# Experts' first layer from seven products for each pair of tiles and pair of blocks, in three passes over the weights

## The chip, the core and the metric

One core of a Trainium2 chip runs the whole program as one launch. The metric is the device time of an execution in microseconds (us). The engines are PE (TensorE: matmuls, with their weight loads shown apart as PEld), DVE (VectorE), ACT (ScalarE), POOL (GpSimd) and SP, which issues the DMAs. Each engine works through its own instructions in a fixed order, and semaphores tell it when an operand is there. PE writes into banks of PSUM, which DVE and ACT read. SBUF holds everything else.

## What is computed

An attention with a threshold, then a gated layer (three weight matrices), then eight dense experts under gates that are normalised over rows and columns in turn. The change is in the experts:

```python
def _moe2_ref(x, w_gate, w1, w2):            # x: 2304 x 512
    logits = x @ w_gate                      # 512 x 8
    P = np.exp(logits - logits.max())
    for _ in range(8):
        P /= P.sum(1, keepdims=True) + 1e-09
        P /= P.sum(0, keepdims=True) + 1e-09
        P *= N / E
    for e in range(E):                       # 8 experts
        h = np.maximum(x @ w1[e], 0.0)       # 512 x 1024
        ye = h @ w2[e]                       # 1024 x 512
        out += P[:, e:e + 1] * ye
```

## The kernel before

Tokens lie in 6 blocks of 384 columns (NBLK, BLK), and a block is 3 tiles of 128 tokens (NTB). A product in full precision is made of three matmuls in fp32r: each operand is split into a high part, which ACT copies (`copy_act`, line 194), and a low part, which DVE or POOL subtracts; `mm3` (lines 853 to 855) then adds high x high, high x low and low x high.

After attention comes the gated layer in `steps` (c, i): four chunks c of the hidden width by six blocks i, with `gate_val` and `down`. The output of block i of the last chunk is `x2[i]`, [128, 4, 384], and `down` splits it for the experts into `x2s[i]` (line 1019). `logits` and `logits_t` make the gates' logits from it.

The experts follow in `steps2`: the 8 x 8 hidden tiles of 128 features go in 24 groups g of three, three and two for each expert, and each group runs over all six blocks. Step (g, i) is `up` (for every hidden tile 12 matmuls of 384 columns into one bank of `ps_a`, a relu on ACT, line 1116, and the low part on DVE, line 1117) and then `mix` of the step before, so that PE does not wait for the relu. `mix` makes, for each of the 3 token tiles, 3 matmuls of 512 columns for every hidden tile of the group into one of the four banks of `ps_o`, and DVE adds the bank to `acc[i]` with the gate (line 1151; without a gate for expert 0, line 1147; where expert 0 is finished, line 1150 multiplies its sum by the gate once). All six `acc` stay in SBUF, and the weights of a group (`a{g}` of w1, `b{g}` of w2) are loaded once, two loads ahead, and split once by `w_step`, which is called between the steps: ACT copies the high part, POOL subtracts the low part (line 799).

`gate_steps` (lines 1071 to 1099) is a generator: it turns the logits into gates in short pieces of DVE work with one small PE matmul between two pieces (`mxT`, `mxB`, eight times `cs`). Two pieces go behind each step from the third step on.

Scratch in SBUF comes from slots of one size (`new`, `drop`, first free first taken).

## Time and profile before

| | |
|---|---|
| median of 3 runs | 2411.72 us (2410.64 to 2414.01) |
| the profiled execution, whole | 2410.57 us |
| its span, from the first to the last instruction | 2408.5 us |
| mean granted TensorE clock | 0.995 |
| PE busy / PEld | 2365.5 us (98%) / 2141.9 us (89%) |
| DVE / ACT / POOL busy | 1097.1 / 652.8 / 628.9 us (46 / 27 / 26%) |
| read from / written to HBM | 68.96 / 7.08 MB |

A page of the profile shows one execution. Matmuls are pipelined: the duration of one is longer than the distance from its start to the start of the next, and it is the distance that counts where they run without a gap. "Idle before" an instruction is time in which its engine had nothing to do. In the span, attention ends at about 350 us, the gated layer runs to about 800 us, and the experts take the rest.

### The profile page before, as it was taken

The numbers are of one execution on the slowest core, as the hardware profiler recorded it, in microseconds if no ns is written. First come the engines' busy times: TensorE is split into PE (matmuls) and PEld (weight loads), VectorE is DVE, ScalarE is ACT, GpSimd is POOL, SyncE is SP. The second block draws the span as 40 slices with busy tenths as digits, with TensorE's granted clock in tenths as the row PEclk, the third lists the DMA queues.
The fourth block names the chain that finished last, engine by engine and source line by source line (L and its number), as shares of the span: only waits on it lengthen the run. The fifth ranks groups of instructions, "written<-read, shape, count | busy, mean of one in ns | idle before, by whom it ended". The sixth has DMA issues, their size and how long they took to land.

```text
span 2408.5 us, 31221 instructions
## 1 busy us (share of the span) xinstructions
PE 2365.5 (98%) x12925; PEld 2141.9 (89%) x12925; DVE 1097.1 (46%) x1873; ACT 652.8 (27%) x1154; POOL 628.9 (26%) x601
## 2 busy tenths in 40 slices
...
DMA packets 94365, 107.40 MB, mean 45 GB/s; under 512 B 45200, under 2 KB 70800, under 8 KB 94224
## 3 DMA queue, kind: packets, MB, share of 16 engines
...
q14 instruction: 40, 0.33, 0.0%
HBM read 68.96 MB, written 7.08 MB: 32 GB/s over the span
## 4 chain that ended last, share of the span: by engine, by line
PE 90%; POOL 5%; issue 1%; DMA 1%; ACT 1%; DVE 1%; SPq 1%; POOLq 0%; DVEq 0%; ACTq 0%
PE h L853 11%; PE h L855 11%; PE h L854 11%; PE y L854 11%; PE y L855 11%; PE y L853 11%; PE d L854 2%; PE d L855 2%; PE d L853 2%; PE v L853 2%; PE v L854 2%; PE v L855 2%; PE g L853 2%; PE g L854 2%; PE g L855 2%; PE s L454 1%
## 5 line engine op out<-in xcount | busy, mean ns | idle before, releaser
L1116 ACT ACTIVATE hh<-h 128x384 fp32r<-128x384 f32 x384 | 188.8, 492 | 1194.8 <-PE h L855 1194.8
L1117 DVE SCALAR_TENSOR_TENSOR hl<-h,hh 128x384 fp32r<-128x384 f32 x384 | 213.9, 557 | 629.4 <-ACT hh L1116 629.3
L1151 DVE SCALAR_TENSOR_TENSOR acc<-y,gate_p,acc 128x512 f32<-128x512 f32 x378 | 283.9, 751 | 357.7 <-PE y L855 357.6
L478 DVE SCALAR_TENSOR_TENSOR em<-ns,st,ee 128x576 f32<-128x576 f32 x144 | 138.3, 960 | 12.6 <-POOL st L465 8.2
L990 POOL TENSOR_TENSOR al<-av,ah 128x384 fp32r<-128x384 f32 x72 | 88.2, 1226 | 179.2 <-ACT ah L194 179.2
L469 ACT ACTIVATE ee<-ns,st 128x576 f32<-128x576 f32 x144 | 111.6, 775 | 32.1 <-DVE ns L461 31.2
L454 PE MATMUL s<-kk,qs 128*128 128x288 f32 x512 | 99.8, 325 | 18.1 <-DMA kk<-khl 9.5
L461 DVE TENSOR_SCALAR_CACHE_REDUCE ns<-s 128x576 f32<-128x576 f32 x144 | 108.3, 752 | 17.2 <-PE s L454 11.2
L988 DVE TENSOR_TENSOR av<-v,s 128x384 f32<-128x384 f32 x72 | 40.0, 556 | 158.9 <-PE v L855 143.3
L454 PEld LDWEIGHTS s<-kk,qs 128*128 128x128 f32 x512 | 75.1, 197 | 38.6 <-DVE ns L461 13.8
L544 PE MATMUL t<-ident,em 128*128 128x128 f32 x576 | 85.6, 280 | 3.1 <-ACT et L194 2.2
L194 ACT ACTIVATE et<-t 128x512 f32<-128x512 f32 x144 | 83.3, 591 | 9.6 <-PE t L544 9.2
L465 POOL TENSOR_TENSOR st<-st,ntau 128x1 f32<-128x1 f32 x144 | 67.9, 471 | 53.4 <-DVE ns L461 52.0
L194 ACT ACTIVATE ah<-av 128x384 fp32r<-128x384 f32 x72 | 37.9, 526 | 158.8 <-DVE av L988 158.8
L544 PEld LDWEIGHTS t<-ident,em 128*128 128x128 f32 x576 | 67.9, 143 | 11.6 <-ACT et L194 5.3
L626 PE MATMUL pv<-et,rv 128*64 128x320 f32 (+1 forms) x512 | 73.7, 421 | 0.7 <-ACT raw_k L383 0.7
L1013 DVE TENSOR_TENSOR x<-d,x 128x384 f32<-128x384 f32 x72 | 39.4, 554 | 35.6 <-PE d L855 35.6
L986 ACT ACTIVATE s<-g 128x384 f32<-128x384 f32 x72 | 34.7, 482 | 75.3 <-PE g L855 75.3
L626 PEld LDWEIGHTS pv<-et,rv 128*64 128x64 f32 x512 | 33.2, 139 | 24.0 <-issue 6.5
L640 POOL TENSOR_TENSOR xT<-u,rb 64x64 f32<-64x64 f32 (+2 forms) x71 | 46.0, 661 | 4.4 <-ACT u L194 3.2
L1147 DVE TENSOR_TENSOR acc<-y,acc 128x512 f32<-128x512 f32 x36 | 24.9, 692 | 32.2 <-PE y L855 32.2
L1019 POOL TENSOR_TENSOR x2l<-x,x2h 128x1536 fp32r<-128x1536 f32 x6 | 21.0, 3503 | 24.6 <-ACT x2h L194 24.6
...
## 6 DMA issues: line engine op xcount, KB each, us to landing
...
raw_a<-in_moe_w_dram SPq DMA_DIRECT2D x16, 768.0 KB, 4.5
raw_b<-in_moe_w_dram SPq DMA_DIRECT2D x16, 768.0 KB, 4.6
...
raw_g<-in_moe_w_gate_dram SPq DMA_DIRECT2D x6, 768.0 KB, 4.7
raw_v<-in_moe_w_val_dram SPq DMA_DIRECT2D x6, 768.0 KB, 4.6
raw_o<-in_moe_w_out_dram SPq DMA_DIRECT2D x6, 768.0 KB, 4.4
...
```

The costliest lines, as they stand in the source:

```text
L194: nc.scalar.activation(out=o, in_=i, func=AF.Copy)
L454: nc.tensor.matmul(ps[:, n, 0:HS], lhs, rhs[:, ko + n * HS:ko + (n + 1) * HS], start=(x == 0), stop=(x == len(ops) - 1))
L461: nc.vector.tensor_scalar(x, sc[t], -1.0, None, op0=ALU.mult, op1=ALU.min, accum_out=stat[t][:, 0:1])
L469: nc.scalar.activation(out=ee[t], in_=sc[t], func=AF.Exp, bias=stat[t][:, 0:1], scale=-1.0)
L478: nc.vector.scalar_tensor_tensor(m, sc.pop(t), stat.pop(t)[:, 1:2], ee.pop(t), op0=ALU.is_le, op1=ALU.mult, accum_out=sums[p][:, s:s + 1],)
L544: nc.tensor.transpose(ps[:, kb * P:(kb + 1) * P], em[p, s // 2][:, o:o + P], ident)
L853: nc.tensor.matmul(ps, a[0], b[0], start=start, stop=False)
L854: nc.tensor.matmul(ps, a[0], b[1], start=False, stop=False)
L855: nc.tensor.matmul(ps, a[1], b[0], start=False, stop=stop)
L1116: nc.scalar.activation(out=hh[:, f], in_=t[:, 0:BLK], func=AF.Relu)
L1117: nc.vector.scalar_tensor_tensor(hl[:, f], t[:, 0:BLK], 0.0, hh[:, f].bitcast(F32), op0=ALU.max, op1=ALU.subtract)
L1151: nc.vector.scalar_tensor_tensor(a, t, gate_p[:, i * NTB + n, e:e + 1], a, op0=ALU.mult, op1=ALU.add)
```

## The change

The experts' first layer now takes two hidden tiles (256 features), two halves of d (2 x 256) and two blocks of tokens together as a product of 2 x 2 matrices, and makes it from seven products in the place of eight (`PARTS`). Each product is 6 matmuls of 384 columns (2 parts of d by the 3 of the split). Its operands are sums: of the weights s1 to s4 (`a_steps`, made anew in every pass on DVE and then split) and of the blocks t1 to t4 (`x_sums`). Some sums of products are made in PSUM, by letting a later product add to a bank whose contents ACT has copied out (`kept`); others on DVE (`hidden`, which adds a bank to a kept copy, so that relu and low part now read SBUF for three of the four tiles).

The loops turn inside out: a step k is one of 32 pairs of hidden tiles (NG) for one pair of blocks u, and there are three passes u = 0, 1, 2 over all weights, so 96 steps. Weights are loaded and split in each pass: `a_load(k + 2)` and `b_load(k)` issue five DMAs at the start of step k; `a_steps(k + 1)` and then `b_steps(k)` are handed out by `w_some` in pieces, two in each `between`. A `between` also issues one token tile of the `mix` of the step before (6 matmuls of 512 columns) and one piece of `gate_steps`. In a step PE thus runs products 1, 2, a token tile, 6, a tile, 5, a tile, 7, a tile, 4, 3 and two tiles. At the turn of a pass three tiles come right behind product 2 (`first`). The operands of the next pass are split in steps 29 and 61 (`x_first`, `x_second`) and summed and split in steps 31 and 63 (`x_sums`); those of the first pass inside the last chunk of the gated layer. Blocks 2 to 5 give their logits by plain fp32 matmuls; block 1 by 12 in the place of 8. Output is stored at the end of each pass.

```diff
-    groups = []
-    for e in range(E):
...
+    PAIRS = FE // P // 2
+    NG = E * PAIRS
...
-    for g, (e, f, n) in enumerate(groups):
...
-            for x in range(2):
-                nc.tensor.matmul(
-                    ps[0:2 * E, 0:BLK], gws[:, c].rearrange("p a e -> p (a e)"), x2s[i][x][:, c, :],
...
+        u, second = divmod(i, 2)
+        n = E if u else 2 * E
+        if u:
+            mms = [(gw[:, c], x2[i][:, c, :]) for c in range(CC)]
...
+    def x_op(u, nm, x, eng):
+        t = new([P, 2, 2, BLK], F32R, f"X{u}_{nm}")
+        xo[u, nm] = hi, lo = t[:, 0], t[:, 1]
+        copy_act(hi, x)
+        eng.tensor_tensor(lo, x, hi.bitcast(F32), op=ALU.subtract)
+    def x_first(u):
+        for nm, c in (("11", 0), ("21", 2)):
+            x_op(u, nm, x2[2 * u][:, c:c + 2, :], nc.gpsimd)
+    def x_second(u):
+        x_op(u, "22", x2[2 * u + 1][:, 2:4, :], nc.gpsimd)
+    def x_sums(u):
+        (b11, b21), (b12, b22) = ((x[:, 0:2, :], x[:, 2:4, :]) for x in x2[2 * u:2 * u + 2])
+        for nm, out, a, b in (("t1", b11, b12, b11), ("t3", b12, b22, b12), ("t2", b22, b22, b11), ("t4", b21, b21, b22)):
+            nc.vector.tensor_tensor(out, a, b, op=ALU.subtract)
+        for nm, x, eng in (("t2", b22, nc.vector), ("t1", b11, nc.gpsimd), ("t3", b12, nc.vector), ("t4", b21, nc.gpsimd)):
+            x_op(u, nm, x, eng)
+        drop(f"x2_{2 * u}")
+        drop(f"x2_{2 * u + 1}")
+    wa, wb, raws = {}, {}, {}
...
+    def a_load(k):
+        e, j = divmod(k % NG, PAIRS)
+        f = 2 * j * P
+        src = w1[e].rearrange("(c p) f -> p c f", p=P)
+        t = raws["a", k] = rw.tile([P, 6, 2, P], F32, tag="raw", name=f"a{k}")
+        nc.sync.dma_start(t[:, 0:2].rearrange("p a c f -> p (a c) f"), src[:, :, f:f + P])
+        nc.sync.dma_start(t[:, 2], src[:, 2:4, f + P:f + 2 * P])
+        nc.sync.dma_start(t[:, 3], src[:, 0:2, f + P:f + 2 * P])
...
+    def a_steps(k):
+        t = raws.pop(("a", k))
+        a11, a12, a22, a21 = (t[:, n] for n in range(4))
+        s1, s2, s3, s4 = t[:, 4], t[:, 5], a21, a12
+        one = new([P, 2, 3, 2, P], F32R, f"wa{k}")
+        two = new([P, 2, 3, 2, P], F32R, f"wb{k}")
+        three = new([P, 2, 2, P], F32R, f"wc{k}")
+        wa[k] = {"s4": (three[:, 0], three[:, 1])}
+        for n, (x, y) in enumerate((("11", "s3"), ("12", "s1"), ("22", "s2"))):
+            wa[k][x] = one[:, 0, n], one[:, 1, n]
+            wa[k][y] = two[:, 0, n], two[:, 1, n]
+        def split(hi, lo, x):
+            yield lambda: copy_act(hi, x)
+            yield lambda: nc.gpsimd.tensor_tensor(lo, x, hi.bitcast(F32), op=ALU.subtract)
+        def sums():
+            nc.vector.tensor_tensor(s1, a21, a22, op=ALU.add)
+            nc.vector.tensor_tensor(s2, s1, a11, op=ALU.subtract)
+            nc.vector.tensor_tensor(s3, a11, a21, op=ALU.subtract)
+        yield sums
+        yield from split(one[:, 0], one[:, 1], t[:, 0:3])
+        yield from split(two[:, 0], two[:, 1], t[:, 3:6])
+        yield lambda: nc.vector.tensor_tensor(s4, a12, s2, op=ALU.subtract)
+        yield from split(three[:, 0], three[:, 1], s4)
...
+    def b_load(k):
+        e, j = divmod(k % NG, PAIRS)
...
+        for n, t in enumerate(raws["b", k]):
+            nc.sync.dma_start(t, w2[e][f + n * P:f + (n + 1) * P, :])
...
+    def b_steps(k):
+        hi, lo = wb[k] = new([P, 2, DM], F32R, f"b{k}h"), new([P, 2, DM], F32R, f"b{k}l")
+        for n, t in enumerate(raws.pop(("b", k))):
+            yield lambda n=n, t=t: copy_act(hi[:, n], t)
+            yield lambda n=n, t=t: nc.gpsimd.tensor_tensor(lo[:, n], t, hi[:, n].bitcast(F32), op=ALU.subtract)
...
             if ip == NBLK - 1:
                 w_drop(f"o{cp}")
-        if c == NCH - 1 and i >= 2:
-            logits(i - 2)
+        if c == NCH - 1:
+            if i == 1:
+                x_first(0)
+            if i == 2:
+                x_second(0)
+                x_sums(0)
+            if i == 4:
+                a_load(0)
+                a_load(1)
+            if i == 5:
+                for fn in a_steps(0):
...
-    def up(g, i):
...
-            sl = slice(f * P, (f + 1) * P)
-            for d in range(CC):
-                mm3(t[:, 0:BLK], (wh[:, d, sl], wl[:, d, sl]), (xh[:, d, :], xl[:, d, :]), d == 0, d == CC - 1)
-            nc.scalar.activation(out=hh[:, f], in_=t[:, 0:BLK], func=AF.Relu)
-            nc.vector.scalar_tensor_tensor(hl[:, f], t[:, 0:BLK], 0.0, hh[:, f].bitcast(F32), op0=ALU.max, op1=ALU.subtract)
...
+    def up(k, u):
...
+        def mm(ps, n, start):
+            a, b = wa[k][PARTS[n][0]], xo[u, PARTS[n][1]]
+            for d in range(2):
+                (ah, al), (bh, bl) = ((x[:, d] for x in y) for y in (a, b))
+                nc.tensor.matmul(ps, ah, bh, start=start and d == 0, stop=False, skip_group_check=True)
+                nc.tensor.matmul(ps, ah, bl, start=False, stop=False, skip_group_check=True)
+                nc.tensor.matmul(ps, al, bh, start=False, stop=d == 1, skip_group_check=True)
...
+        def kept(ps, tag):
+            t = tmp.tile([P, BLK], F32, tag=tag, name=tag)
+            copy_act(t, ps)
+            return t
+        def hidden(nm, x, ps=None):
+            if ps is not None:
+                nc.vector.tensor_tensor(x, ps, x, op=ALU.add)
+            if nm in ("11", "22"):
+                for m in (nm, "21" if nm == "11" else "12"):
+                    hid[k, u, m] = hp_.tile([P, 2, BLK], F32R, tag="h", name=f"h{k}_{u}_{m}")
+            h = hid[k, u, nm]
+            nc.scalar.activation(out=h[:, 0], in_=x, func=AF.Relu)
+            nc.vector.scalar_tensor_tensor(h[:, 1], x, 0.0, h[:, 0].bitcast(F32), op0=ALU.max, op1=ALU.subtract)
+        a = bank()
+        mm(a, 1, True)
+        p1 = kept(a, "s")
+        yield
+        b = bank()
+        mm(b, 2, True)
+        hidden("11", p1, b)
+        yield
+        mm(a, 6, False)
+        u2 = kept(a, "av")
+        yield
+        c = bank()
+        mm(c, 5, True)
+        yield
+        mm(a, 7, False)
+        u3 = kept(a, "u3")
+        hidden("22", u3, c)
+        yield
+        mm(a, 4, False)
+        hidden("21", a)
+        yield
+        mm(c, 3, False)
+        hidden("12", u2, c)
+        yield
...
-    def mix(g, i):
...
+    def mix(k, u):
...
+            if g == 0 and n == 0:
...
-            for f in range(nf):
-                mm3(t, (hh[:, f, sl], hl[:, f, sl]), (wh[:, f], wl[:, f]), f == 0, f == nf - 1)
+            for f, h in enumerate(hs):
+                mm3(t, (h[:, 0, sl], h[:, 1, sl]), (wh[:, f], wl[:, f]), f == 0, f == 1)
...
-    steps2 = [(g, i) for g in range(NG) for i in range(NBLK)]
+                if n == NTB - 1:
+                    drop(f"acc{i}")
+            yield
+    steps2 = [(k, k // NG) for k in range(3 * NG)]
     sink = None
-    for n, (g, i) in enumerate(steps2):
-        for _ in range(2):
...
-        up(g, i)
...
-            logits_t(NBLK - 2)
...
+    def between(n):
+        nonlocal sink
+        x = next(fill, None)
+        if callable(x):
+            x()
+        w_some(n)
+        if sink is not None and next(sink, 0) == 0:
+            sink = None
+    for k, u in steps2:
+        if k + 2 < len(steps2):
+            a_load(k + 2)
+        b_load(k)
+        products = up(k, u)
+        fill = iter([down_last, lambda: logits(4)]) if k == 0 else mix(*steps2[k - 1])
+        if k + 1 < len(steps2):
+            w_parts.extend(a_steps(k + 1))
+        if k == 5:
+            while sink is not None:
+                between(0)
+        first = k and u > steps2[k - 1][1]
+        next(products)
+        next(products)
+        between(2)
+        if first:
+            between(1)
+            between(1)
+        next(products)
+        if not first:
+            between(2)
+        next(products)
+        between(2)
+        next(products)
+        between(2)
+        next(products)
+        next(products)
+        w_parts.extend(b_steps(k))
+        a_drop(k)
+        if k % NG == NG - 3 and u < 2:
+            x_first(u + 1)
+            x_second(u + 1)
+        if k % NG == NG - 1 and u < 2:
+            for nm in ("11", "21", "22", "t1", "t2", "t3", "t4"):
+                drop(f"X{u}_{nm}")
+            x_sums(u + 1)
+        between(2)
+        between(2)
+        w_some(99)
...
+            logits_t(4)
+        if k == 1:
+            logits_t(5)
             sink = gate_steps()
-        if sink is not None:
-            for _ in range(2):
-                if next(sink, 0) == 0:
-                    sink = None
-                    break
-    mix(*steps2[-1])
+    for _ in mix(*steps2[-1]):
+        pass
```

What is left out are the same edits elsewhere: hidden tiles of the gated layer are single tiles [128, 2, 384] of a pool of six, in the place of two tiles of three, and the weights of the experts are no longer in the list of `pieces`.

What stands in a row on DVE in the middle of the experts, ahead (`hl`: low part of a hidden tile; `acc`: a token tile is added):

```order
L1117 SCALAR_TENSOR_TENSOR hl12_1_14302<-h12_1_0_14303,hh12_1_14301 128x384
L1117 SCALAR_TENSOR_TENSOR hl12_1_14302<-h12_1_1_14318,hh12_1_14301 128x384
L1117 SCALAR_TENSOR_TENSOR hl12_1_14302<-h12_1_2_14333,hh12_1_14301 128x384
L1151 SCALAR_TENSOR_TENSOR acc0_8884<-y12_0_0_14348,gate_p_8722,acc0_8884 128x512
L1151 SCALAR_TENSOR_TENSOR acc0_8884<-y12_0_1_14359,gate_p_8722,acc0_8884 128x512
L1151 SCALAR_TENSOR_TENSOR acc0_8884<-y12_0_2_14370,gate_p_8722,acc0_8884 128x512
L1117 SCALAR_TENSOR_TENSOR hl12_2_14382<-h12_2_0_14383,hh12_2_14381 128x384
```

And now, from the first token tile of step 20 on (`a21`: the sums of step 21's weights; `u3` and `av`: kept copies of a bank):

```order
L1289 SCALAR_TENSOR_TENSOR acc0_8932<-y19_0_0_11721,gate_p_8735,acc0_8932 128x512
L1074 TENSOR_TENSOR a21_11548<-a21_11548 128x256
L1075 TENSOR_TENSOR a21_11548<-a21_11548 128x256
L1076 TENSOR_TENSOR a21_11548<-a21_11548 128x256
L1289 SCALAR_TENSOR_TENSOR acc0_8932<-y19_0_1_11741,gate_p_8735,acc0_8932 128x512
L1289 SCALAR_TENSOR_TENSOR acc0_8932<-y19_0_2_11758,gate_p_8735,acc0_8932 128x512
L1081 TENSOR_TENSOR a21_11548<-a21_11548 128x256
L1221 TENSOR_TENSOR u3_11774<-up20_0_11751,u3_11774 128x384
L1228 SCALAR_TENSOR_TENSOR h20_0_22_11777<-u3_11774,h20_0_22_11777 128x384
L1289 SCALAR_TENSOR_TENSOR acc1_8993<-y19_1_0_11781,gate_p_8735,acc1_8993 128x512
L1228 SCALAR_TENSOR_TENSOR h20_0_21_11718<-up20_0_11700,h20_0_21_11718 128x384
```

Between the additions of token tiles there now stand the sums of the weights, the additions of products, and low parts that read SBUF alone.

On POOL, in the middle of the experts, one split of a group's weights followed the other, two for every six blocks:

```order
L799 TENSOR_TENSOR a12l_13862<-raw_a12_13373,a12h_13861 128x1536
L799 TENSOR_TENSOR b12l_13933<-raw_b12_13459,b12h_13932 128x1536
L799 TENSOR_TENSOR a13l_14219<-raw_a13_13865,a13h_14218 128x1536
L799 TENSOR_TENSOR b13l_14296<-raw_b13_13936,b13h_14295 128x1536
L799 TENSOR_TENSOR a14l_14702<-raw_a14_14222,a14h_14701 128x1024
```

Now, at the end of the first pass, in steps 29 to 31 (`wa`, `wb`, `wc`: split weights of w1; `X1`: split blocks of the next pass):

```order
L1071 TENSOR_TENSOR wc30_12968<-a30_12817,wc30_12968 128x256
L1024 TENSOR_TENSOR X1_11_13079<-x2_2_5458,X1_11_13079 128x768
L1024 TENSOR_TENSOR X1_21_13082<-x2_2_5458,X1_21_13082 128x768
L1024 TENSOR_TENSOR X1_22_13085<-x2_3_5606,X1_22_13085 128x768
L1100 TENSOR_TENSOR b29l_13078<-b29_0_12962,b29h_13077 128x512
L1100 TENSOR_TENSOR b29l_13078<-b29_1_12963,b29h_13077 128x512
```

Five such splits belong to every step, and at the turn of a pass the splits of the blocks stand ahead of those of w2.

## Rows read from the trace of the kernel before

**Rows 1.** Busy time by stretch: length, PE, PEld, DVE, ACT, POOL, clock, DMA, GB/s.
```profile
1000.00:1200.00 200.00, 200.00 (x1016) 182.40 (x1015) 75.03 (x120) 31.50 (x55) 18.80 (x6) 1.00 0.07 22
```
**Rows 2.** What PE waited for from 800 us on: us, times, longest.
```profile
PE mxT L1077 <- DVE sx L1074: 1.3, 1, 1.3
```
**Rows 3.** Tile view: min/median/max ns, first and last start, of two groups' matmuls.
```profile
L853 PE MATMUL h<-x2h,a3h x72: 333/334/346, 1006.9 to 1072.8; 128*128 128x384 f32 x72
...
L853 PE MATMUL h<-x2h,a21h x72: 333/334/346, 2200.7 to 2266.5; 128*128 128x384 f32 x72
```
**Rows 4.** Timeline, one step of the experts: start us, us, engine, what.
```profile
1503.28 0.33 PE L853 MATMUL h<-x2h,a10h 128*128 128x384 f32 x1
...
1504.15 0.33 PE L855 MATMUL h<-x2h,a10l 128*128 128x384 f32 x1
...
1504.52 0.49 ACT L1116 ACTIVATE hh<-h 128x384 fp32r<-128x384 f32 x1 [7.77 <-PE h L855]
...
1505.04 0.56 DVE L1117 SCALAR_TENSOR_TENSOR hl<-h,hh 128x384 fp32r<-128x384 f32 x1 [1.88 <-ACT hh L1116]
...
1508.31 0.33 PE L855 MATMUL h<-x2h,a10l 128*128 128x384 f32 x1
```
**Rows 5.** Groups of DVE, ACT and PE instructions: count, busy us, mean ns, idle before.
```profile
L1151 DVE SCALAR_TENSOR_TENSOR acc<-y,gate_p,acc 128x512 f32<-128x512 f32 x378 | 283.9, 751 | 357.7 <-PE y L855 357.6
...
L1150 DVE TENSOR_SCALAR acc<-acc,gate_p 128x512 f32<-128x512 f32 x18 | 9.6, 532 | 0.0
...
L1116 ACT ACTIVATE hh<-h 128x384 fp32r<-128x384 f32 x384 | 188.8, 492 | 1194.8 <-PE h L855 1194.8
L194 ACT ACTIVATE ah<-av 128x384 fp32r<-128x384 f32 x37 | 19.4, 525 | 78.8 <-DVE av L988 78.8
...
L194 ACT ACTIVATE v3h<-cv 128x768 fp32r<-128x768 f32 x2 | 1.7, 840 | 4.0 <-DVE cv L832 4.0
...
L1094 PE MATMUL cs<-cs,ones 128*128 128x8 f32 x16 | 2.3, 214 | 0.0
```
**Rows 6.** Views of single tiles and lines: min/median/max ns, first and last start.
```profile
L988 DVE TENSOR_TENSOR av<-v,s x72: 544/558/558, 353.1 to 790.1; 128x384 f32<-128x384 f32 x72
...
L395 POOL TENSOR_TENSOR qthl<-raw_qt,qthl x15: 453/462/1059, 24.3 to 293.5; 128x128 fp32r<-128x128 f32 x15
...
L876 POOL TENSOR_TENSOR s_0l<-xT,s_0h x4: 989/1000/1462, 70.0 to 131.3; 128x384 fp32r<-128x384 f32 x4
...
L876 POOL TENSOR_TENSOR w<-stage,w x6: 1275/1294/1782, 316.6 to 329.9; 128x512 fp32r<-128x512 f32 x6
...
L799 POOL TENSOR_TENSOR o3l<-cv,o3h x2: 1841/1944/2048, 691.9 to 707.8; 128x768 fp32r<-128x768 f32 x2
```
**Rows 7.** Timeline: POOL and DVE instructions with two inputs in SBUF.
```profile
587.00 0.95 DVE L831 TENSOR_TENSOR raw_o<-raw_o 128x768 f32<-128x768 f32 x1
...
893.34 2.40 POOL L799 TENSOR_TENSOR b2l<-raw_b,b2h 128x1024 fp32r<-128x1024 f32 x1 [77.03 <-ACT b2h L194]
...
893.68 2.22 DVE L1089 TENSOR_TENSOR gate_p<-gate_p,rs 128x144 f32<-128x144 f32 x1
```
**Rows 8.** Timeline of DVE: two pieces of the gates, first, eighth and last instruction.
```profile
866.52 0.17 DVE L1095 TENSOR_SCALAR cs<-cs 128x8 f32<-128x8 f32 x1 [5.21 <-PE cs L1094]
...
868.36 0.31 DVE L1089 TENSOR_TENSOR gate_p<-gate_p,rs 128x144 f32<-128x144 f32 x1
868.70 0.43 DVE L1091 TENSOR_REDUCE cs<-gate_p 128x8 f32<-128x144 f32 x1
```
**Rows 9.** Chain that ended last: start us, us; a stretch of fp32 matmuls of 256 columns.
```profile
10.08 1.74 PE warm L301 x8
```
**Rows 10.** Timeline: last matmul and last addition of the program.
```profile
2403.49 0.39 PE L855 MATMUL y<-b23h,hl 128*128 128x512 f32 x1
2403.92 0.75 DVE L1151 SCALAR_TENSOR_TENSOR acc<-y,gate_p,acc 128x512 f32<-128x512 f32 x1 [0.61 <-PE y L855]
```
**Rows 11.** The page's DMA issues: count, KB each, median us to landing.
```profile
raw_a<-in_moe_w_dram SPq DMA_DIRECT2D x16, 768.0 KB, 4.5
```

130 lines of the change are left out of this document (62 added, 68 removed).

## Prediction

> **What bounds the kernel now.** I read the busy time by stretch first: in the experts PE is busy for 200.00 of 200 us, DVE for 75, ACT for 32, POOL for 19, at a granted clock of 1.00 [rows 1]. Then what PE waited for from 800 us on: one wait, 1.3 us [rows 2]. So the experts last as long as their matmuls are apart, and no other engine sets anything. The distances: from the first to the last of 30 matmuls of 384 columns in a row it is 5.03 us, so 0.1735 us for one [rows 4]. Groups 3 to 20 are 288 pairs of a hidden tile and a block, each with 12 such matmuls and 9 of 512 columns; from the start of group 3 to that of group 21 it is 1193.8 us [rows 3], so 4.145 us for a pair, and (4.145 - 12 x 0.1735) / 9 = 0.229 us for a matmul of 512 columns.
>
> **What the change removes.** 4608 matmuls of 384 columns become 96 steps x 7 products x 6 = 4032. 576 x 0.1735 = **99.9 us**, all on the path. The second layer keeps its 3456 matmuls. A new step is 42 x 0.1735 + 36 x 0.229 = 15.54 us of PE. Nothing else shrinks, so the question is how much of the 100 us comes back as waits of PE, which had none.
>
> **A step in the middle of a pass.** Its work on the other engines, by rows. DVE: 6 additions of token tiles at 0.751 [rows 5], 7 instructions on 384 columns at 0.556 (PSUM and SBUF: `av` [rows 6]; low parts 0.56 [rows 4]), 4 sums of 256 columns at 0.42 (on the line through 144 columns at 0.31 [rows 8] and 768 at 0.95 [rows 7]): 10.1 us. ACT: 4 from PSUM at 0.49, 3 from SBUF at 0.525, splits of 2 x 768, 256 and 2 x 512 columns at 0.84, 0.42 and 0.63 (line through 384 at 0.525 and 768 at 0.840) [rows 5]: 6.9 us. POOL: 2 x 1.84 + 2 x 1.28 + 0.73 (256 columns, between 128 and 384) [rows 6]: 7.0 us. All are under 15.54, so none becomes the bound by its sum; what can hurt is the order.
>
> I laid the step out in that order, with 0.37 us from the start of a product's last matmul until ACT begins on the bank, which is 0.20 us after the next matmul may start, and 0.03 us from ACT to DVE [rows 4]. Times are from the start of product 1: products 1 and 2, tile 1 at 2.08, product 6 at 3.46, tile, product 5 at 5.87, tile, product 7 at 8.29, tile, product 4 at 10.71, product 3 at 11.75, tiles 5 and 6 from 12.79. The kept copies are out of their banks in time: product 4 needs the copy behind product 7, which is done at 10.1. The tight chain is the split of w2, which the next step's tile 1 reads. Product 3 can be read at 13.0; DVE comes to it at 13.8; addition to 14.4, relu to 14.9, high part of the first half to 15.5, POOL's two low parts to 16.8 and 18.1. Tile 1 of the next step needs the second half with its fifth matmul, at 15.54 + 2.08 + 4 x 0.229 = 18.5. **Slack 0.4 us, stall 0** in the 80 or so plain steps.
>
> DVE comes late to product 3 because of POOL. With POOL at work on two inputs from SBUF, DVE's product of two SBUF tiles took 2.22 us [rows 7], where the same instruction takes 0.31 [rows 8]: it ended only behind POOL's 2.40 us. An input from PSUM takes no such harm: `av` never took over 0.558 us [rows 6] though POOL was busy for half of that stage. I take it that such a pair excludes each other. In the old experts POOL worked 19 us in 200 [rows 1] and DVE read PSUM, so it cost nothing. Now POOL works 7.0 us in each step, and seven DVE instructions of a step read SBUF alone (four sums, three low parts). In the layout s4 waits for POOL until 10.25, and everything behind it on DVE moves by some 0.8 us. The Trainium skill, "SBUF — State Buffer", section "Who interferes with whom", says the same as a rule: a DVE instruction with two SBUF inputs and a GpSimd instruction that reads SBUF take a shared port in turn, each for its whole length. That is the rule that speaks against this change; without it the sum below would be the first rival's 2363.
>
> **Where waits do come back**, each laid out by the same rows:
>
> - The first pass, steps 1 to 6: **+32 us**. A pair of gate pieces is 2.61 us of DVE (866.52 to 869.13 [rows 8]); steps 2 to 4 take three pairs each, so DVE has 17.6 us and some 40 starts for a step of 15.54, and `cs` on PE now stands one tile behind the DVE piece that feeds it, where it stood a whole step behind. At least 17.6 - 15.54 = 2 us a step; laid out, +4.5, +7.7 and +7.7. Step 5 takes the last pieces and the six multiplications by the gate (0.53 [rows 5]) with their tiles: +6; step 6 clears the queue, +4; step 1 +2. Bounds 6 (DVE's sum alone in three steps) and 45.
> - The turns of the passes: **2 x 16 us**. In steps 29 and 61 three splits of 768 columns (3 x 1.84 on POOL) stand ahead of that of w2: its low parts come 5.5 us later, tile 1 waits 5.1. In steps 31 and 63 four sums of 768 columns (4 x 0.98 with the start) delay DVE, four copies of 0.84 ACT, and two splits and DVE's two low parts POOL: the second half of w2 is ready at some 27.4 in place of 18.1, and tile 1 waits 9.7; the step behind adds a little. The three tiles in a row behind product 2 cover the sums themselves but not this. Bounds 2 x 10 and 2 x 20.
> - Steps 37, 38, 69 and 70, multiplications by the gate in the later passes: **+7 us** (0 to 14).
> - Logits: an fp32 matmul takes 0.218 us in 256 columns for each record, 8 in 1.74 us [rows 9], and such a matmul shows two records (16 for the eight `cs` [rows 5]); in 384 columns 0.65 us. Four blocks at 4 x 0.65 in place of 8 x 0.1735, and 4 more matmuls for block 1: **+5.6 us**.
> - Step 0 has no tile between products 7 and 4, so PE waits for the kept copy: **+1**. Behind step 95 the last `mix` has no products ahead of it and waits for w2's split, 18.1 - 15.54 less four matmuls: **+2**.
>
> At nothing I cost: the DMAs (five a step, 1 MB; 0.75 MB landed in 4.5 us [rows 11], rows of 512 bytes may double that; w1 has over a step, w2 has 10 us; SP is free); `x_sums` in the gated layer (6 us of DVE and ACT, while PE has two tiles' products, 8.3 us, in banks ahead; if that cover fails, 2 to 4 us); slots (eight are free, so one is written at the earliest a step after its last reader). The end is as now: the last addition starts 0.43 us behind the last matmul [rows 10].
>
> Sum: -99.9 + 32 + 32 + 7 + 5.6 + 1 + 2 = **-20 us**. The profiled execution, 2410.57 us with 2.1 us outside its span of 2408.5, would come to 2390.3; it lies 1.15 us under the median of 2411.72, so the forecast against the median is **2391 us**.
>
> **Rivals.** *The waits overlap better* (DVE and POOL don't exclude each other for low parts, or the queues give way): laid out without the exclusion, the first three terms are 19 + 24 + 0 in place of 71, so 28 less: **2363**. For it: the evidence is from few pairs. Against: rows 7 are plain.
>
> *Every step waits* (slower). Place: tile 1 of each step, for w2's second low part. It decides once that chain is over 0.4 us later than laid out; from there each 0.1 us costs 95 x 0.1 = 9.5 us, and 0.17 us a step more eat the 16 us by which the forecast is over 0.2% faster. POOL's 512 columns are 1.28 in the middle but up to 1.78 [rows 6], and each DVE start may cost 0.03 more; with 1.4 us, 2.0 for 768 columns and those starts, the plain steps lose 0.25 on average and the rest grows by 12: +35, **2426**. For it: the three engines hand over to each other four times in this chain, and the cover is 0.4 us of 5. Against: every duration in the layout is a median of its row, and the handovers are in it.
>
> *Products cost more than 0.1735 a matmul.* A step changes 10 times between 384 and 512 columns, and each product may begin with a wait. In the old step the change at 1508.31 cost nothing; at 0.03 us each it is 96 x 10 x 0.03 = 29 us: **2420**.
>
> That fewer matmuls are issued is certain from the order (4032), so "it does not do what it says" is none.
>
> **How the numbers follow.** Forecast 0.52 (own range 2376 to 2408), better overlap 0.16 (2352 to 2375), every step waits 0.20 (2408 to 2460), dearer products 0.12 (2402 to 2440). The range is 2360 to 2433: it leaves out the lower third of the second case (0.05), and of the slower ones half of the third case (0.10) and a little of the fourth (0.02). A measurement of this kernel can tell about 0.2%, 4.8 us, from no change: faster means under 2407, slower over 2416.5. By the four cases in turn, faster: 0.50 + 0.16 + 0 + 0.01 = 0.67; same: 0.02 + 0 + 0.04 + 0.04 = 0.10; slower: 0.16 + 0.07 = 0.23.
>
> **What would show it.** In the changed profile: 4032 matmuls of 384 columns in the experts, 0.1735 apart; plain steps 15.5 us long with no wait of PE for a `b` low part (over 0.3 us there is the second rival); steps 2 to 4 of 20 to 23 us with PE waiting for `cs`; waits of 5 and 10 us for w2's low parts behind steps 29, 31, 61 and 63; DVE low parts from SBUF of 1 to 2.5 us beside POOL. I would be wrong if PE waits in places the layout has none, for product 6 or 4 above all, or if a DMA lands late.

## The result and the profile after

The changed kernel takes **2385.39 us** (median of 4 runs, 2384.81 to 2386.10), the kernel before beside it 2411.18 us (4 runs, 2409.43 to 2414.01): ratio 0.9897, 95% interval 0.9884 to 0.9909. The forecast was 2391 us; 4608 - 4032 matmuls less are worth 4.1% by the working, and 1.0% came.

The page of the kernel after: busy time of the engines, share of the span and instructions.

```profile
span 2384.3 us, 33858 instructions
...
PE 2301.3 (97%) x12353; PEld 2049.6 (86%) x12353; DVE 1656.6 (69%) x2707; ACT 1028.5 (43%) x1889; POOL 1167.0 (49%) x1043
```

DVE has half as much again to do as before (1097.1 us), POOL nearly twice (628.9), and PE 64 us less, of which the span shows 24. What PE waited for from 780 us on, the largest of it (us, times, longest):

```profile
PE cs L1185 <- DVE cs L1182: 10.9, 5, 3.4
PE y L845 <- POOL b29l L1100: 4.2, 2, 3.9
PE y L845 <- POOL b61l L1100: 3.9, 1, 3.9
PE y L844 <- ACT b31h L194: 3.5, 1, 3.5
PE y L844 <- ACT b63h L194: 3.5, 1, 3.5
PE y L845 <- POOL b31l L1100: 3.2, 1, 3.2
PE y L845 <- POOL b63l L1100: 2.9, 1, 2.9
```

Where [rows 2] had one wait of 1.3 us, there are now the gates' rounds and, at each turn of a pass, w2's two parts. Busy time by stretch shows what that costs; a stretch is a step, from its product 1 to the next one's (length, PE, PEld, DVE, ACT, POOL, clock, DMA, GB/s). In order: steps 2, 3 and 4; 20, a plain one; 30; 32.

```profile
836.90:855.39 18.49, 16.74 (x86) 14.55 (x85) 10.98 (x24) 8.50 (x16) 6.72 (x5) 1.00 0.19 59
855.39:878.63 23.24, 18.38 (x85) 15.98 (x84) 19.11 (x46) 6.71 (x14) 7.04 (x6) 0.93 0.17 47
878.63:908.51 29.88, 23.05 (x99) 18.68 (x98) 25.72 (x62) 6.70 (x13) 9.48 (x7) 0.91 0.20 53
...
1145.78:1161.42 15.64, 15.64 (x80) 14.07 (x78) 11.35 (x17) 6.48 (x12) 7.04 (x6) 1.00 0.23 69
...
1302.18:1323.98 21.80, 17.60 (x80) 15.24 (x78) 10.76 (x17) 8.11 (x16) 12.84 (x9) 0.92 0.18 51
...
1339.62:1364.83 25.21, 18.55 (x80) 15.44 (x78) 15.83 (x23) 9.40 (x17) 11.53 (x7) 0.86 0.22 75
```

The plain step is PE from end to end, as in [rows 1]. In steps 30 and 32 PE is busy for 2.0 and 2.9 us longer with the same matmuls, at a lower granted clock: a wait costs its own length and then something behind it. Steps 3 to 6 show the same, at granted clocks of 0.93, 0.91, 0.94 and 0.91; the forecast has no term for it.

By the steps' lengths, against the terms of the sum (us):

| term | forecast | measured |
|---|---|---|
| 576 matmuls fewer, at 0.1735 | -99.9 | -99.9 by the count |
| 96 plain steps, 15.64 in place of 15.54 | 0 | +9.6 |
| steps 1 to 6 (16.1, 18.5, 23.2, 29.9, 14.0, 19.9) over 6 x 15.64 | +32 | +27.8 |
| two turns: steps 30, 32, 33 (21.8, 25.2, 15.9) and 62, 64, 65 (22.2, 25.4, 15.9) | +32 | +32.6 |
| steps 37, 38, 69, 70 (16.05, 16.8, 16.0, 16.8) | +7 | +3.1 |
| logits, step 0, last `mix`: the rest | +8.6 | +2.6 |
| the spans' difference | -20.3 | -24.2 |

The forecast put steps 5 and 6 at +6 and +4; the code makes all gate pieces that are left, and two of step 5's token tiles with them, ahead of product 1 of step 5, so step 4 has them (+14.2) and step 5 is short (-1.6). The sum of the six is what compares. The experts start between 797.4 and 803.5 us in the profiled executions of the changed kernel and its variants, with the same code ahead of them, so the steps' lengths tell small effects better than the times.

The row "the rest" is what is left of the difference of two executions, and it holds more than its name says. Read one by one in PE's timeline, the logits cost 5.9 us (four fp32 matmuls take 2.68 in place of 8 x 0.1735, for four blocks, and block 1 has four matmuls more), the wait for the kept copy in step 0 costs 0.6, and those of the last `mix` 0.4: 6.9 in all. Against them stands what the kernel before spent on its own gates, for which the forecast has no term: its group 3 starts 209 us behind its first matmul of the experts, by an estimate from its distances some 4 us more than its pairs, its logits and its last `down` take.

### The profile page after: what moved, and what is told of

Its sections match the earlier page's. It is cut to its first block, busy times and chain, and to the rows that moved or that the text cites. A ratio compares the mean times of both kernels' runs of the same rounds, so it can differ in the third digit from the quotient of the medians.

```text
span 2384.3 us, 33858 instructions
## 1 busy us (share of the span) xinstructions
PE 2301.3 (97%) x12353; PEld 2049.6 (86%) x12353; DVE 1656.6 (69%) x2707; ACT 1028.5 (43%) x1889; POOL 1167.0 (49%) x1043
## 3 DMA queue, kind: packets, MB, share of 16 engines
q1 hardware_dynamic: 203536, 172.56, 26.6%
HBM read 136.07 MB, written 7.08 MB: 60 GB/s over the span
## 4 chain that ended last, share of the span: by engine, by line
PE 82%; POOL 5%; DVE 5%; issue 3%; DMA 2%; SPq 1%; ACT 1%; POOLq 0%; DVEq 0%; ACTq 0%
PE y L845 11%; PE y L846 10%; PE y L844 10%; PE up L1208 9%; PE up L1207 9%; PE up L1209 9%; PE d L846 2%; PE d L845 2%; PE d L844 2%; PE v L844 2%; PE v L846 2%; PE v L845 2%; PE g L844 2%; PE g L846 2%; PE g L845 2%
## 5 line engine op out<-in xcount | busy, mean ns | idle before, releaser
L1289 DVE SCALAR_TENSOR_TENSOR acc<-y,gate_p,acc 128x512 f32<-128x512 f32 x504 | 376.4, 747 | 112.8 <-PE y L846 110.4
L1071 POOL TENSOR_TENSOR wa<-a,wa 128x768 fp32r<-128x768 f32 x96 | 177.4, 1848 | 232.6 <-ACT wa L194 230.5
L1071 POOL TENSOR_TENSOR wb<-a,wb 128x768 fp32r<-128x768 f32 x96 | 177.7, 1851 | 204.7 <-ACT wb L194 201.6
L1208 PE MATMUL up<-X_t,wb 128*128 128x384 f32 x576 | 195.5, 339 | 0.0
L1207 PE MATMUL up<-X_t,wb 128*128 128x384 f32 x576 | 194.3, 337 | 0.0
L1209 PE MATMUL up<-X_t,wb 128*128 128x384 f32 x576 | 193.8, 336 | 0.0
L989 POOL TENSOR_TENSOR h<-av,h 128x384 fp32r<-128x384 f32 x72 | 89.1, 1239 | 198.0 <-ACT h L194 198.0
L1071 POOL TENSOR_TENSOR wc<-a,wc 128x256 fp32r<-128x256 f32 x96 | 77.2, 804 | 191.4 <-ACT wc L194 188.0
L194 ACT ACTIVATE wb<-a 128x768 fp32r<-128x768 f32 x96 | 81.2, 846 | 196.2 <-DVE a L1076 190.7
L1074 DVE TENSOR_TENSOR a<-a 128x256 f32<-128x256 f32 x96 | 155.6, 1620 | 0.0
L1207 PE MATMUL up<-X,wa 128*128 128x384 f32 x384 | 130.0, 338 | 0.0
L1209 PE MATMUL up<-X,wa 128*128 128x384 f32 x384 | 129.7, 338 | 0.0
L1208 PE MATMUL up<-X,wa 128*128 128x384 f32 x384 | 129.3, 337 | 0.0
L1208 PEld LDWEIGHTS up<-X_t,wb 128*128 128x128 f32 x576 | 109.2, 190 | 13.4
L1207 PEld LDWEIGHTS up<-X_t,wb 128*128 128x128 f32 x576 | 109.2, 190 | 12.5 <-issue 0.6
L461 DVE TENSOR_SCALAR_CACHE_REDUCE ns<-s 128x576 f32<-128x576 f32 x144 | 108.4, 752 | 12.6 <-PE s L454 6.3
```

Source lines behind the costliest of these rows:

```text
L194: nc.scalar.activation(out=o, in_=i, func=AF.Copy)
L1071: yield lambda: nc.gpsimd.tensor_tensor(lo, x, hi.bitcast(F32), op=ALU.subtract)
L1074: nc.vector.tensor_tensor(s1, a21, a22, op=ALU.add)
L1207: nc.tensor.matmul(ps, ah, bh, start=start and d == 0, stop=False, skip_group_check=True)
L1208: nc.tensor.matmul(ps, ah, bl, start=False, stop=False, skip_group_check=True)
L1209: nc.tensor.matmul(ps, al, bh, start=False, stop=d == 1, skip_group_check=True)
```

## Experiments

The theory in the forecast: PE's matmuls set a plain step; what comes back is waits in a few steps, for two reasons, DVE full with the gates in steps 1 to 6 (made worse by POOL, which excludes DVE), and w2's low parts behind the splits and sums of blocks at the turns.

### Is a plain step bound by PE?

Product 3 is made twice, which leaves the other engines their work.

```diff
         mm(c, 3, False)
+        mm(c, 3, False)
```

> The changed kernel with product 3 made twice into its bank (the experts' result is then another; 6 more matmuls in each of 96 steps, nothing else added), so PE does the work of eight products. Theory (plain steps are bound by PE at 0.1735 us a matmul): + 96 x 6 x 0.1735 = +99.9 us, less up to 5 for waits that the product covers: one time of 2480 to 2487. Rival (part of the seven-for-eight gain was lost because products cost more than their matmuls, by waits or by changing shape): over 2495. Rival (plain steps are bound by another engine): under 2460.

Measured: 2478.36 us (one run), +93.0 and 1.6 us under the theory's range. A plain step takes 16.68 us, +1.04 = 6 x 0.1735, and PE is busy for all of it. Step 20:

```profile
1161.10:1177.78 16.68, 16.68 (x86) 15.11 (x84) 11.44 (x17) 6.48 (x12) 7.05 (x6) 1.00 0.22 64
```

Over 96 steps that is 99.8. Of what is missing some 5 us went into steps that wait anyway (3.3 in steps 1 to 6, 1.0 in step 38 and 1.0 in step 70), and in this execution the experts start 2.2 us earlier. A matmul more costs its distance at once, so PE is the bound in plain steps.

### How much slack has w2's chain in a plain step?

The rival "every step waits" decided at 0.4 us. POOL makes the low part of w2's first half three times.

```diff
-            yield lambda n=n, t=t: nc.gpsimd.tensor_tensor(lo[:, n], t, hi[:, n].bitcast(F32), op=ALU.subtract)
+            def low(n=n, t=t):
+                for _ in range(1 if n else 3):
+                    nc.gpsimd.tensor_tensor(lo[:, n], t, hi[:, n].bitcast(F32), op=ALU.subtract)
+            yield low
```

> The changed kernel with the low part of w2's first half subtracted three times on POOL (the same result, 2 x 1.28 us more for POOL in each step, at the tightest chain). By the changed kernel's trace the second low part is there 1.2 us before the matmul that reads it: then each of about 91 steps waits 2.58 - 1.22 = 1.36 us, +124 us, a time of 2500 to 2520. By the layout of the prediction the slack was 0.4: 2.58 - 0.43 = 2.15 us, +196 us, 2570 to 2590. If this chain decides nothing: under 2400.

Measured: 2556.54 us (one run). POOL's timeline: the low parts of w2 ahead of a plain step, first those ahead of step 20 in the kernel after, then those ahead of step 18 here; and step 18 here.

```profile
1145.05 2.54 POOL L1100 TENSOR_TENSOR b19l<-b,b19h 128x512 fp32r<-128x512 f32 x2 [2.31 <-ACT b19h L194]
```
```profile
1136.27 5.25 POOL L1102 TENSOR_TENSOR b17l<-b,b17h 128x512 fp32r<-128x512 f32 x4 [2.43 <-ACT b17h L194]
```
```profile
1137.05:1154.31 17.26, 16.20 (x80) 13.96 (x78) 10.88 (x17) 6.48 (x12) 9.88 (x8) 1.00 0.22 62
```

The chain takes 2.71 us longer, and a plain step grows by 1.62 (17.26 for 15.64): the slack is 2.71 - 1.62 = **1.1 us**, not 0.4. The trace after says nearly the same: POOL ends at 1145.05 + 2.54 = 1147.59, and the fifth matmul of tile 1 in step 20, which reads the second low part, starts at 1148.81, 1.2 us behind. The total lies between both expectations. Of the 171 us 96 x 1.62 are 156; the other 15 are the sum of steps that grew by more (33, 34, 38, 65, 66, 70 and the end) and of steps 1 to 6, which grew by only 5.4 in all. The rival's mechanism is real (the wait for `b` low parts appears in every step, 1.1 us in two parts, and PE is busy for 0.56 us more), but its point lies nearly three times as far off as forecast. A reason can be read in DVE's timeline of step 20 after, though no run tests it: an instruction starts before the recorded end of the one ahead, where the layout had put 0.03 us between them.

```profile
1157.70 0.75 DVE L1289 SCALAR_TENSOR_TENSOR acc<-y,gate_p,acc 128x512 f32<-128x512 f32 x1
1158.40 0.56 DVE L1228 SCALAR_TENSOR_TENSOR h<-up,h 128x384 fp32r<-128x384 f32 x1
1158.88 0.55 DVE L1221 TENSOR_TENSOR av<-up,av 128x384 f32<-128x384 f32 x1
```

1157.70 to 1158.40 is 0.70 for a duration of 0.75, and 0.48 for 0.56. The addition to product 3's bank (`av`, 1158.88) is 13.1 us behind product 1 (1145.78); the layout had 13.8.

### What does the exclusion of DVE by POOL cost?

The low parts of the first layer's weights come from ACT as copies; readers and waits stay.

```diff
-            yield lambda: nc.gpsimd.tensor_tensor(lo, x, hi.bitcast(F32), op=ALU.subtract)
+            yield lambda: copy_act(lo, x)
```

> The low parts of the first layer's weights come from ScalarE as plain copies (left out: the subtraction, so the low part is the whole weight) and no longer from POOL. Every reader and every wait for them stays. It measures what POOL's and VectorE's exclusion costs. Theory (POOL's subtraction holds VectorE's sums of weights up: 1.77 us in place of 0.42 and 1.15 in place of 0.42, 2.1 us per step; it costs nothing in a plain step, since PE is the bound, and prolongs the steps in which VectorE is full, 1 to 6): the sums fall to 0.42 us, plain steps stay at 15.64, steps 1 to 6 fall from 121.7 to 108 to 114 us in all, the turns by 0 to 3 us each: 2371 to 2380 us. Rival (steps 1 to 6 are long through the gate's chain between PE and VectorE alone): they stay within 2 us of 121.7, 2383 to 2387 us.

Measured: 2373.22 us (2 runs), 12.2 under the changed kernel, as the theory has it. The group of the first sum of weights in the kernel after, and in this one (count, busy us, mean ns):

```profile
L1074 DVE TENSOR_TENSOR a<-a 128x256 f32<-128x256 f32 x96 | 155.6, 1620 | 0.0
```
```profile
L1074 DVE TENSOR_TENSOR a<-a 128x256 f32<-128x256 f32 x96 | 39.9, 416 | 0.0
```

Same instruction, four times as long beside POOL's `wa` subtraction. In the kernel after it finds POOL at work in 87 of the 96 steps; there it takes 1.75 us and ends 0.28 us behind POOL, and where POOL is idle it takes 0.42. The Trainium skill, "SBUF — State Buffer", section "Who interferes with whom", says that a DVE instruction with two SBUF inputs and a GpSimd instruction that reads SBUF hold a shared port in turn; these durations agree.

The low parts, which the forecast expected at 1 to 2.5 us, took no such harm. Two of the three from SBUF in the kernel after (shortest, median and longest in ns):

```profile
L1228 DVE SCALAR_TENSOR_TENSOR h<-s,h x96: 557/558/1744, 803.8 to 2357.9; 128x384 fp32r<-128x384 f32 x96
L1228 DVE SCALAR_TENSOR_TENSOR h<-u,h x96: 557/558/560, 816.4 to 2365.7; 128x384 fp32r<-128x384 f32 x96
```

Only 5 of the 288 find POOL at work when they start. So what is held up is the first sum and s4 (1.03 us on average), not the low parts: that much of the first rival, that the low parts escape, was right. The multiplications by the gate, with one tile from SBUF as input, are held up too, here in the kernel after and in this one:

```profile
L1288 DVE TENSOR_SCALAR acc<-acc,gate_p 128x512 f32<-128x512 f32 x18 | 14.9, 826 | 0.0
```
```profile
L1288 DVE TENSOR_SCALAR acc<-acc,gate_p 128x512 f32<-128x512 f32 x18 | 9.0, 499 | 0.0
```

Steps 1 to 6 fall from 121.7 to 109.1 us, steps 37, 38, 69 and 70 to 15.64, plain steps stay at 15.64, and the turns stay (22.7 and 25.7; 21.5 and 25.1). Steps 3 and 4 here:

```profile
855.31:874.58 19.27, 16.84 (x86) 14.58 (x84) 16.32 (x45) 8.14 (x16) 2.54 (x2) 1.00 0.19 56
874.58:900.66 26.08, 20.94 (x100) 16.84 (x98) 22.70 (x61) 8.84 (x17) 5.05 (x4) 1.00 0.21 60
```

So the exclusion is real. Taking off the first layer's part of POOL's work (4.5 of 7.0 us a step) saves 12.6 us in steps 1 to 6 and 3.1 in the four others, and nothing in plain steps. The forecast had put 28 us on it: 13 in steps 1 to 6, 8 at the turns, where nothing is saved, and 7 in steps 37, 38, 69 and 70. Nor is all of the 12.6 time that DVE waits: the granted clock is 1.00 here where it was 0.93 and 0.91, and PE itself is busy for 5.8 us less in steps 1 to 6. The run also shortens POOL's queue, so by itself it doesn't tell the two apart; the last run below does, in which POOL has more to do and DVE less.

### How much of steps 1 to 6 is the gates' rounds?

The eight rounds are left out.

```diff
-        for _ in range(8):
+        for _ in range(0):
```

> The eight rounds of normalising the gates are left out (the gates are then the exponentials alone); the logits, the maximum and everything else stay. It measures what of the 28.4 us, by which steps 1 to 6 are longer than six plain ones, is the gates' rounds. If all of it: steps 1 to 6 fall to 94 to 96 us in all, 2357 to 2360 us. If the sums of weights and the accumulators already fill VectorE there: they stay at 100 us or more, above 2363 us.

Measured: 2361.96 us (2 runs), steps 1 to 6 in all 98.8 us, both between the two expectations: 22.8 of the 27.8 us are the rounds. Steps 3 and 4 become plain (15.64). What is left is 2.6 in step 2, where PE waits 1.8 us for the logits' maximum, 0.5 in step 1, and 0.75 and 1.1 in steps 5 and 6, where DVE multiplies the accumulators by the gate, as in steps 37 and 38.

### Can the rounds be handed out better?

PE's `cs` matmul stands one tile behind the DVE piece that feeds it. Here two pieces go out at every second call, so that it has two tiles.

```diff
-        if sink is not None and next(sink, 0) == 0:
-            sink = None
+        if sink is not None:
+            calls[0] += 1
+            for _ in range(1 if calls[0] < 3 else 2 * (calls[0] % 2)):
+                if sink is not None and next(sink, 0) == 0:
+                    sink = None
```

> The changed kernel with the pieces of the gates handed out in pairs at every second place (the second half of one round and the first half of the next together), so that the small PE matmul of a round stands two token tiles behind the DVE piece that feeds it, not one. DVE's work is the same. Theory (waits come from where a thing stands in the order): PE's waits for cs, 10.9 us in the changed kernel, fall under 2, and the whole time falls from 2385.4 to some 2376 (2373 to 2380); steps 2 to 4 stay longer than 15.6 us, because DVE has 17 us of work in them. Rival (steps 2 to 6 are long because DVE and POOL are full, wherever PE waits for it): the waits move to other matmuls, 2383 to 2387.

Measured: 2382.78 us (2382.14 to 2385.56), ratio 0.9883 (0.9867 to 0.9900), 2.6 under the changed kernel and nearer to the rival's number than to the theory's. The wait is nearly as long as before:

```profile
PE cs L1185 <- DVE cs L1182: 9.4, 4, 3.9
```

Steps 1 to 6 take 116.8 us, 4.8 less. The rival was right in the main, though the wait stayed at `cs` and did not move to other matmuls: it is less the distance of `cs` from its source than DVE's work that decides (its busy time in step 3 is 20.06 us, where a plain step has 15.64).

### The turns

At a turn the splits and sums of the next pass stand ahead of the tile's own w2 split on ACT and POOL. Here they are handed out behind it.

```diff
-        if k % NG == NG - 3 and u < 2:
-            x_first(u + 1)
...
-            x_sums(u + 1)
         between(2)
         between(2)
         w_some(99)
+        if k % NG == NG - 3 and u < 2:
+            x_first(u + 1)
...
+            x_sums(u + 1)
```

> The changed kernel with the splits and sums of the next pass's blocks (steps 29, 31, 61, 63) issued behind the two last token tiles and behind the split of w2, not ahead of them. The work is the same. Theory (the turn costs 2 x 16 us because w2's low parts stand behind the blocks' splits): the four waits at the first token tile, 3.9 + 6.7 + 3.9 + 6.4 us, go; a new wait of 2 to 3 us at product 6 of steps 32 and 64 comes, for the copy of product 1, which now stands behind four copies on ACT; the whole time is 2385.4 less 20 to 28: 2357 to 2366. Rival (POOL and DVE simply have 10 us more to do there): less than 8 us is won, 2378 to 2386.

Measured: 2373.19 us (2370.87 to 2374.77), ratio 0.9840 (0.9825 to 0.9855). That is 12.2 us won, between the theory's 20 to 28 and the rival's 8. Step 30 falls from 21.8 to 17.6, but step 32 only from 25.2 to 22.7: a turn still costs 9.4 us of its 16. The waits for `b31` and `b63` are gone, and others stand in their place:

```profile
PE up L1207 <- ACT av L194: 5.0, 2, 3.3
PE up L1207 <- ACT s L194: 3.5, 2, 1.8
```

ACT's timeline in step 32, which starts at 1337.82, has their source:

```profile
1342.48 3.05 ACT L194 ACTIVATE X_t<-x 128x768 fp32r<-128x768 f32 x4 [5.00 <-DVE x L1038]
1345.43 0.47 ACT L194 ACTIVATE s<-up 128x384 f32<-128x384 f32 x1
```

The four copies wait 5 us for DVE's four subtractions, and the copy of product 1, before which product 6 can't add to its bank, stands behind them. The copy of product 6 (`av`) comes late in the same way, at 1352.47, behind the copy for `wb`.

So the subtractions, which need nothing of the last steps, go one step ahead (`x_split` is the second half of `x_sums`):

```diff
+        if k % NG == NG - 2 and u < 2:
+            x_sums(u + 1)
         if k % NG == NG - 1 and u < 2:
...
-            x_sums(u + 1)
+            x_split(u + 1)
```

> The later turn (products' own splits handed out behind the tile's work) left 9.4 us at each change of pass, 1.8 and 3.3 us of it in PE's waits for ACT's copies of a product, because ACT's four copies of the X sums (3.05 us) stood in the queue ahead of them and were themselves late: they waited for VectorE's four subtractions of blocks. Here these four subtractions (4 x 0.96 us, they need nothing of the last steps) are made one step earlier, beside the work of step 30 and 62, and only the splits stay at the turn. Theory (the copies are late because the subtractions are): ACT has its four copies done by the end of product 1, both waits go, steps 32/33 and 64/65 fall from 22.7 to 16 to 17.5 us, steps 31 and 63 rise by 0 to 1: 2359 to 2365 us. Rival (VectorE has no room for 3.9 us in any one step, so the wait is only moved one step ahead): steps 31 and 63 take 18 to 19 us, 32/33 fall to 18: 2367 to 2372 us.

Measured: 2370.0 us (2365.39 to 2374.90), ratio 0.9833 (0.9816 to 0.9851). Step 32 falls to 17.9, step 31 rises to 18.5: the rival's numbers. Of the 4.9 us that step 32 gives back, 2.8 return in step 31: DVE, busy there for 16.49 us, has no room for 3.9 us in one step. The four times scatter by 9.5 us, more than this run wins, so the steps' lengths carry the reading.

### Both cures together, and spread further

The gate's pieces in twos, the early subtractions, and the splits of blocks 11 and 21 one step ahead of that of block 22.

> The early subtractions, with the two splits of the first operands also taken apart (the pair of blocks 11 and 21 in step 29 and 61, block 22 in step 30 and 62), and with the gate's rounds handed out two pieces at every second call. If the three causes add up: what the early subtractions give, less 2 x 1.5 us (steps 30 and 62, 17.6 us so far, fall to 16), less the 2.6 us that the gate's pairs gave alone: 5 to 6 us under the early subtractions' time, 2353 to 2361 us. If the splits of block 11, 21 and 22 cost the same wherever they stand (POOL at 2.2 us each behind w2's low parts), only the gate's pairs show: 2 to 3 us under it.

Measured: 2359.24 us (2358.74 to 2360.19), ratio 0.9790 (0.9773 to 0.9806). Steps 1 to 6 take 116.8, 4.9 less than in the run before, where the pairs alone gave 4.8; step 30 falls to 15.64, and with what steps 29 and 61 take on (0.3 and 0.5) the two turns give 3.0, as expected. By the steps' lengths the parts add up; the medians differ by 10.8 us, more than that, because those of the run before scatter.

Then each subtraction and each split in a step of its own, from step 24 of a pass on:

```diff
+        if u < 2:
+            for n, fn in enumerate((lambda: x_first(u + 1), lambda: x_second(u + 1), lambda: x_sums(u + 1, ("t1",)),
+                                    lambda: x_sums(u + 1, ("t3",)), lambda: x_sums(u + 1, ("t2",)), lambda: x_sums(u + 1, ("t4",)))):
+                if k % NG == NG - 8 + n:
+                    fn()
```

> The kernel with all three cures (2359 us) still takes 18.2 us in steps 31 and 63, in which VectorE makes four subtractions of blocks (4 x 0.96 us, 1.7 us where POOL works beside it). Here each of the four has a step of its own, and so have the splits of blocks 11 and 21 and of block 22, from step 24 to step 29 of a pass. Theory (a step's VectorE has room for about one subtraction): step 31 falls to 15.7, the steps that get one take 15.6 to 16.1: 2 x 1 to 2 x 2.5 us less, 2354 to 2357 us. Rival (each subtraction costs its time wherever it stands, since sums of weights, low parts and accumulators stand in a fixed order behind it): what step 31 loses comes back in the four steps, 2358 to 2361 us.

Measured: 2355.96 us (2354.50 to 2356.70), ratio 0.9780 (0.9766 to 0.9795). Step 31 falls from 18.2 to 15.64 and the steps that got a subtraction or a split take 15.64 to 16.2. A plain step has room for one of them.

Last, three of the four sums of weights on POOL for the first eight tiles:

```diff
-            nc.vector.tensor_tensor(s1, a21, a22, op=ALU.add)
-            nc.vector.tensor_tensor(s2, s1, a11, op=ALU.subtract)
-            nc.vector.tensor_tensor(s3, a11, a21, op=ALU.subtract)
+            eng = nc.gpsimd if k < 8 else nc.vector
+            eng.tensor_tensor(s1, a21, a22, op=ALU.add)
+            eng.tensor_tensor(s2, s1, a11, op=ALU.subtract)
+            eng.tensor_tensor(s3, a11, a21, op=ALU.subtract)
```

> The same, with three of the four sums of the first layer's weights on POOL for the first eight tiles (built in steps 0 to 7), where VectorE is full with the gates. Theory (VectorE is what is short in steps 1 to 6; without POOL's low parts these six steps took 109.2 us in place of 121.7): VectorE loses 0.42 + 0.42 + 0.42 us a step and up to 1.35 us of waiting for POOL, steps 1 to 6 fall from 116.8 to 108 to 113 us: 4 to 9 us under the spread version. Rival (POOL gets 2.4 us a step more, its low parts come later and its hold on VectorE lasts as long): steps 1 to 6 take 115 to 122 us, 2 us less to 5 more than the spread version.

Measured: **2349.73 us** (2349.05 to 2351.44), ratio 0.9756 (0.9740 to 0.9772), the fastest here and 35.7 us under the changed kernel (34 by the two ratios, each to the kernel before beside it). Its steps 3 and 4:

```profile
856.14:877.17 21.03, 17.15 (x85) 14.56 (x84) 18.37 (x42) 6.15 (x13) 9.26 (x9) 1.00 0.18 48
877.17:902.86 25.69, 19.50 (x94) 15.63 (x92) 22.75 (x52) 6.26 (x13) 13.66 (x13) 1.00 0.26 71
```

Steps 1 to 6 take 110.8 us in place of 117.0, at a clock of 1.00 throughout, though POOL is busier in them: it is DVE that is short there, not POOL's queue. What is left over plain steps: 17.0 in steps 1 to 6, 2.0 in steps 32 and 33 (17.3 and 15.9) and 0.5 in steps 25 and 28, about as much at the second turn, and 1.6 in steps 37 and 38 and again in 69 and 70. No run tried to make the gates' rounds at another place than beside the first steps of the experts.

## Why the forecast was right

**What bounds the kernel, and what is removed: right.** The plain step is PE alone, and six more matmuls cost 6 x 0.1735.

**The distances: a little too small.** A step of 42 and 36 matmuls takes 15.64 us for the 15.54 of the working. In step 20 twelve matmuls of 384 columns go from 1145.78 to 1147.88, 0.175 each, and six of 512 from there to 1149.27, 0.2317 each (0.1735 and 0.229 in the working):

```profile
1145.78 0.33 PE L1207 MATMUL up<-X,wa 128*128 128x384 f32 x1
...
1147.88 0.39 PE L844 MATMUL y<-b19h,h 128*128 128x512 f32 x1
...
1149.27 0.33 PE L1207 MATMUL up<-X_t,wb 128*128 128x384 f32 x1
```

That is the rival "dearer products": 96 x 0.10 = 9.6 us where it had 29. Most of it lies in the matmuls of 512 columns, and the kernel before shows it already, behind the change at 1508.31 that the forecast read as costing nothing:

```profile
1508.48 0.39 PE L853 MATMUL y<-b10h,hh 128*128 128x512 f32 x1
...
1509.87 0.39 PE L853 MATMUL y<-b10h,hh 128*128 128x512 f32 x1
...
1511.24 0.39 PE L853 MATMUL y<-b10h,hh 128*128 128x512 f32 x1
...
1514.64 0.33 PE L853 MATMUL h<-x2h,a10h 128*128 128x384 f32 x1
```

The first six behind the change are 0.2317 apart, as in the new step; the last 15 of the 27 only 0.2267. The mean of 0.229 mixes both, and the new step has its tiles one or two at a time, so it never gets to the shorter distance. A change thus costs 0.03 us, spread over the matmuls behind it, but the working's mean held about half of it already. Why a matmul soon behind a change costs more, no run tells.

**Steps 1 to 6: right in cause and in the sum** (+27.8 for +32), not step by step (step 4 alone has 14.2). It is DVE's load in the main: without the rounds 22.8 of it goes, without POOL's subtractions 12.6, with three sums taken from DVE 6.2 (117.0 to 110.8), and with `cs` further from its source only 4.8. Two parts are not DVE's load. In step 2 DVE is busy for only 10.98 of 18.49 us, and PE waits 1.7 for the logits' maximum; and in steps 3 to 6 some of the time is the granted clock, which the forecast had left out. The 17.6 us that it gives DVE in steps 2 to 4 is not the sum of its rows either: 10.1 + 3 x 2.61 is 17.9, and the 0.3 less fits the first expert's additions, which have no gate (0.692 us in the kernel before), a price that stands in none of them.

**The turns: right in place and in sum (2 x 16.3 for 2 x 16), one part missing.** The low parts of b31 are there when POOL ends, 1347.73 + 2.81 = 1350.54, 26.6 us behind product 1 of step 31 (1323.98); the layout had 27.4. POOL's line, and PE's timeline of tile 1 in step 32:

```profile
1347.73 2.81 POOL L1100 TENSOR_TENSOR b31l<-b,b31h 128x512 fp32r<-128x512 f32 x2
```
```profile
1345.40 0.50 PE L844 MATMUL y<-b31h,h 128*128 128x512 f32 x1 [3.51 <-ACT b31h L194]
...
1349.05 0.79 PE L845 MATMUL y<-b31l,h 128*128 128x512 f32 x1 [3.15 <-POOL b31l L1100]
1349.64 0.63 PE L846 MATMUL y<-b31h,h 128*128 128x512 f32 x1
1350.07 0.63 PE L844 MATMUL y<-b31h,h 128*128 128x512 f32 x1
1350.60 0.80 PE L845 MATMUL y<-b31l,h 128*128 128x512 f32 x1
1351.19 0.63 PE L846 MATMUL y<-b31h,h 128*128 128x512 f32 x1
1351.62 0.63 PE L844 MATMUL y<-b31h,h 128*128 128x512 f32 x1
```

Undisturbed, the fifth matmul would start at 1339.62 + 2.09 + 4 x 0.231 = 1342.6; it starts at 1350.60, 8.0 us late. The rest of the 9.6 us by which this step is long is the matmuls behind it, 0.43 us apart in place of 0.23. In step 30 the two parts are 4.7 (5.1 in the forecast) and 1.5. So the waits came out 1.7 and 0.4 us smaller than forecast. Of the 1.7 some 0.8 is a slip in the forecast's own sum: w2 ready at 27.4 for a matmul at 18.5 is a wait of 8.9 us, not 9.7. The clock, which the forecast had left out, made up for both. That the sum fits so well is in part luck.

**The multiplications by the gate** (+3.1 for +7) come from the same exclusion, as the run with POOL's subtractions taken off shows; the price was too high. **The fp32 logits, step 0 and the last `mix`**: by the timeline 5.9, 0.6 and 0.4 for 5.6, 1 and 2, so the logits were right and the two waits too dear; the +2.6 in the table is lower because the kernel before had some 4 us of its own for the gates.

**Signs.** Steps 2 to 4 were to take 20 to 23 us and took 18.5, 23.2 and 29.9; low parts were to take 1 to 2.5 us and took 0.56. What holds DVE up beside POOL is the sums of weights and the multiplications by the gate.

**The total.** 2385.4 for 2391 is nearer than the parts: against the forecast the plain steps are 9.6 us dearer, steps 1 to 6, the gate's multiplications and the rest 4.2, 3.9 and 6.0 cheaper. That these cancel is luck; the bound, the places and the two large terms are not.

**The slack of w2's chain** (1.1 us for 0.4) was the step on which the slower rival hung, and it was mis-sized, as far as DVE's timeline tells, by DVE's starts. With 1.1, "every step waits" deserved less than its 0.20.

**Costed at nothing.** The new DMAs were: a quarter MB of `a`, in rows of 512 bytes, lands in 2.9 us and one of `b`, in rows of 2 KB, in 2.7, so the doubling that the forecast allowed for did not come, and PE waits for none, though 136.07 MB are read in place of 68.96. The `kept` copies and the bank of product 4 cost nothing in plain steps.
